# An FFT convolution with a gated expert: spectrum stored as row-pair tiles with real and imaginary parts on the free axis, corner turns scattered on the write, and the first spectrum started beside kernel generation

## Chip, cores, metric

The kernel runs on 1 core of one Trainium2 chip. The metric is device microseconds of one execution. A number called "span" is the length of the profiled execution inside the trace; the device time of the same execution is about 2 us more. Engines: PE is the matrix engine, PEld its weight loads, DVE VectorE, ACT ScalarE, POOL GpSimdE, SP SyncE (here it only issues transfers).

## The reference

```python
def reference(u, A, B, C, log_dt, Dskip, w_r, w_gate, w_up, w_down):   # u: 1 x 2048 x 512, names shortened
    xn = layernorm(u)
    # S4 convolution: K[d, l] = Re sum_n C dt B exp(dt A l), then y = irfft(rfft(xn) * rfft(K)) + xn * Dskip
    s = s4_by_fft(xn, ...)
    # the token with the largest xn @ w_r goes through one SwiGLU expert, its row is updated
    upd = scatter(silu(x_sel @ w_gate) * (x_sel @ w_up) @ w_down * sigmoid(r))
    return u + s * silu(xn + upd)
```

The work has these parts, whose names return below. **Generation** makes K on DVE (chains GG, TT; products QQ) and PE, and copies it to tile KT. The **K turn** writes KT to DRAM and reads it back as KT2. The **forward FFT** takes XN0 to AT, through DRAM to BT, and to U2. A **spectrum** (one for each half of the 512 columns, 8 groups each) multiplies KT2 by the table W into PSUM (a K product), copies that to K2T, multiplies by U2 on DVE into PAB, applies the inverse table FA (an inverse product), copies to ZT and writes that to DRAM; DD reads it back, turned. The **expert** gives UPD (its output row) and OTM (where it goes). A **gate** is silu(XN0 + UPD at its row); a **tail** finishes the inverse FFT, adds the skip term XN0 x Dskip, multiplies by the gate and adds the residual XR. There are 8 gates and a first and a last tail.

## The kernel before

Every operation is entered in a graph, and a list scheduler written in the kernel gives each engine a fixed order. A bias raises an operation's priority. The order is static: an engine whose next instruction waits does nothing else. Memory and PSUM banks are also dependences: an operation that overwrites something waits for its last reader. PSUM is the memory that PE writes its products to; the kernel uses eight banks of it, in four pairs.

```python
            cand = [n for n in avail[e] if ready[n.i] <= t]
            n = max(cand, key=lambda n: n.bl + n.bias)       # bl: longest path to the end
```

```python
        AT = place("AT", [128, 2, 8, 512], BF16)
        o_b = cur[0]
        BT = place("BT", [128, 2, 33, 256], BF16)
        F2T = place("F2T", [128, 32, 128], BF16)
        end_u = cur[0]
        W = place("W", [128, 32, 5, 128], BF16, o_u)            # over AT and BT
        FA = place("FA", [128, 32, 2, 128], BF16, o_u + 40960)
        ...
        U2S = [place(f"U2S{h}", [128, 32, 256], BF16) for h in range(2)]
```

```python
        # forward FFT, after kernel generation
            g.dma(SP, [(dap(SA, 8 * pc * 512, [[32 * 512, 128], [1, 4096]]), sap(AT, ...))])       # contiguous write
        ...
                    pr.append((sap(BT, 64 * ri + 32 * bp, 32, ...),                                # 512-byte gather
                               dap(SA, ..., [[512, 32], [32 * 512, nm], [1, 256]])))
        ...
        g.dma(AC, [(FA[:], t_fa.ap()...)])
        for h in range(2):                                       # halves (Re, Im) swapped across partitions
            g.dma(SP, [(U2S[h][0:64, :, :], U2[64:128, h, :, :]), (U2S[h][64:128, :, :], U2[0:64, h, :, :])])

        def spec(h, tg):
            pp = tg % 2
            ...   # 20 K products into PSUM pair pp, copied to K2T
            us = (U2[:, h, 4 * tg:4 * tg + 4, :], U2S[h][:, 4 * tg:4 * tg + 4, :])
            for x in range(2):
                po = PAB[:, pp, x]
                g.V(lambda e, x=x, po=po: e.tensor_tensor(out=po, in0=us[x], in1=ko, op=ALU.mult), ...)
            for t4 in range(4):
                for x in range(2):
                    mms.append((o, FA[:, t, x, :], PAB[:, pp, x, t4, :], x == 0, x == 1))   # 128 rows
            ...   # copied to ZT; one write of ZT for two groups

        def zturn(h):
            pr = []
            for bp in range(2):
                for ri in range(2):
                    pr.append((sap(DD[h], 64 * bp + 32 * ri, 32, 0, [[256, 32], [1, 256]]),
                               dap(SZ[h], (64 * ri + 32 * bp) * 32 * 256, [[256, 32], [32 * 256, 32], [1, 256]])))
            g.dma(SP, pr)
```

Of the kernel before, what the change touches and what calls it, by code (L numbers as in the profile page):

```python
# [49 lines left out]
class _Graph:  # L50
# [3 lines left out]
    def __init__(self, nc):  # L54
        self.nc = nc
        self.ctx = ExitStack()
        self.nodes = []
        self.active = []
        self.dram_bits = {}
        self.ndram = 0  # L60
        self.cache = {}
        self.sbuf = {}

# [64 lines left out]
    def add(self, eng, fns, outs, ins, ns, lat=0.0, dma=False, nbytes=0, bias=0.0, after=(), name=""):  # L128
# [45 lines left out]
    def V(self, fn, outs, ins, n, mode=1, **kw):  # L174
        return self.add(DV, [fn], outs, ins, (60 + n / mode) / 0.96, **kw)

    def A(self, fn, outs, ins, n, **kw):
        return self.add(AC, [fn], outs, ins, 230 + 0.833 * n, **kw)

    def M(self, mms, **kw):  # L180
        fns, outs, ins, ns = [], [], [], 0.0
        for o, l, r, st, sp in mms:
            tp = (_pstart(l), _pstart(o))
            fns.append(lambda e, o=o, l=l, r=r, st=st, sp=sp, tp=tp: e.matmul(o, lhsT=l, rhs=r, start=st, stop=sp, tile_position=tp, skip_group_check=True))  # L184
# [5 lines left out]
            ns += max(58.0, nn / 2.0)  # L190
        return self.add(PE, fns, outs, ins, ns, lat=60.0, **kw)

    def dma(self, eng, pairs, **kw):
        fns, outs, ins = [], [], []
        nd = 0
        nb = 0
        for dst, src in pairs:
# [6 lines left out]
            run = list(dst.ap)[-1][1] if list(dst.ap)[-1][0] == 1 else 1  # L204
            run2 = list(src.ap)[-1][1] if list(src.ap)[-1][0] == 1 else 1
            nd += cnt // max(1, min(run, run2))
            nb += cnt * mybir.dt.size(dst.dtype)
        return self.add(eng, fns, outs, ins, 60.0 * len(pairs) + 1.3 * nd, dma=True, nbytes=nb, **kw)

    def schedule(self):  # L210
# [5 lines left out]
        for n in reversed(nodes):  # L216
            t = n.ns + n.lat + (2000.0 + n.nbytes / 250.0 if n.dma else 60.0)
            n.bl = t + max([s.bl for s in succ[n.i]], default=0.0)
# [10 lines left out]
        while done < len(nodes):  # L229
# [14 lines left out]
            if n.dma:  # L244
                dma_free = max(dma_free, n.end) + n.nbytes / 250.0
# [102 lines left out]

def _pstart(ap):
# [3 lines left out]
def _tables():  # L353
# [30 lines left out]
    ONES = np.zeros((128, 128))  # L384
    ONES[0] = 1.0
    T["cf"] = [("IDENTF", IDENT), ("ONESF", ONES), ("LIDXB", LIDXB), ("CF", CF)]
# [4 lines left out]
    F2T = np.zeros((128, 32, 128))  # L391
    FA = np.zeros((128, 32, 2, 128))
    for t in range(32):
        if t == 0:
            ka, kb = 64 * k1, 32 + 64 * k1
        else:
            ka, kb = t + 64 * k1, (64 - t) + 64 * k1
        for half, kk in ((0, ka), (1, kb)):
            a = tp * np.outer(l1r, kk) / P
            c, s = np.cos(a), np.sin(a)  # L400
            sg = -1.0 if (half == 1 and t > 0) else 1.0
            isr = (ri == 0)[:, None]
            F2T[:, t, 32 * half:32 * half + 32] = np.where(isr, c, sg * s)
            F2T[:, t, 64 + 32 * half:96 + 32 * half] = np.where(isr, -s, sg * c)
        if t == 0:
            F2T[:64, 0, 64] = (-1.0) ** l1r[:64]
            F2T[64:, 0, :] = 0.0
        kin = np.concatenate([ka, kb])
        ang = tp * np.outer(kin, l1r[:64]) / P
        c, s = np.cos(ang), np.sin(ang)  # L410
        if t > 0:
            cj = np.concatenate([np.ones(32), -np.ones(32)])[:, None]
            FA[:64, t, 0, :64] = c
            FA[64:, t, 0, :64] = -c
            FA[:64, t, 1, :64] = -s
            FA[64:, t, 1, :64] = -s
            FA[:64, t, 0, 64:] = cj * s
            FA[64:, t, 0, 64:] = -cj * s
            FA[:64, t, 1, 64:] = cj * c
            FA[64:, t, 1, 64:] = cj * c  # L420
        else:
            for half in range(2):
                rr = slice(32 * half, 32 * half + 32)
                ri_ = slice(64 + 32 * half, 96 + 32 * half)
                co = slice(64 * half, 64 * half + 64)
                FA[rr, 0, 0, co] = c[rr]
                FA[ri_, 0, 0, co] = -c[rr]
                FA[rr, 0, 1, co] = -s[rr]
                FA[ri_, 0, 1, co] = -s[rr]
            FA[0, 0, 0, :64] *= 0.5  # L430
            FA[0, 0, 1, :] = 0.0
            FA[64, 0, 0, :] = 0.0
            FA[64, 0, 1, :] = 0.0
            FA[64, 0, 0, :64] = 0.5 * (-1.0) ** l1r[:64]
# [9 lines left out]
    W = np.zeros((128, 32, 5, 128))  # L444
    for t in range(32):
        if t == 0:
            ka, kb = 64 * k1, 32 + 64 * k1
        else:
            ka, kb = t + 64 * k1, (64 - t) + 64 * k1
        kin = np.concatenate([ka, kb])  # L450
        ang = tp * ((ls[:, None] * kin[None, :]) % P) / P
        full = np.concatenate([np.cos(ang), -np.sin(ang)], axis=1)
        if t == 0:
            full[:, 64] = (-1.0) ** ls
        for l in range(L):
# [3 lines left out]
            W[rr, t, tt] += full[l]  # L459
# [4 lines left out]
def build(nc, A_u, A_A_re, A_A_im, A_B_re, A_B_im, A_C_re, A_C_im, A_log_dt, A_Dskip,  # L464
# [21 lines left out]
    SA = g.dram("scr_a", 128 * 32 * 512)  # L486
    SK = [g.dram(f"scr_k{h}", 128 * 32 * 64) for h in range(2)]
    SKE = [g.dram(f"scr_e{h}", 256) for h in range(2)]
    SZ = [g.dram(f"scr_z{h}", 128 * 32 * 256) for h in range(2)]

    with g.ctx:
        cur = [0]

        def place(name, shape, dt, off=None):
# [3 lines left out]
            nb = (nb + 63) // 64 * 64  # L498
# [5 lines left out]

        XN0 = place("XN0", [128, 16, 512], BF16)
        o_u2 = cur[0]
        U2 = place("U2", [128, 2, 32, 256], BF16)
        KT2 = place("KT2", [128, 2, 5, 256], BF16)
        KT = place("KT", [128, 2, 33, 64], BF16)
# [664 lines left out]
```

## Time and profile before

| | before |
|---|---|
| device time, median of 3 | 304.55 us (303.21 to 305.95) |
| span of the profiled execution | 301.4 us |
| busy PE / DVE / ACT | 159.4 / 171.7 / 141.5 us |

No engine is busy for more than 57% of the span, so the share of busy time decides nothing; the stages do. The first fence is the page of the kernel before: the busy line, and the span cut into 40 slices of 7.5 us (a digit is the busy share in tenths; PEclk is the clock granted to PE in tenths of full speed; DMA is the mean share of the 16 DMA engines).

```profile
PE 159.4 (53%) x2067; PEld 98.3 (33%) x2067; DVE 171.7 (57%) x437; ACT 141.5 (47%) x158; POOL 0.2 (0%) x4
...
DVE  1699599999999992479650000030144446356073
...
PEclk9999999999995555855875799659789999975555
DMA  8999700000000002086899959999856649837925
```

DVE is nearly full in slices 3 to 15, while DMA does nothing from slice 6 to 15; in slices 22 to 28 DMA is full and DVE nearly idle. The next fence is the table by stage of the kernel before (start:end in us, length, busy us of each engine with its number of instructions, granted clock, DMA share, GB/s).

```profile
8.00:110.00 102.00, 32.30 (x566) 20.09 (x566) 95.49 (x282) 44.51 (x51) 0.00 (x0) 0.91 0.31 79
...
162.00:215.00 53.00, 33.02 (x323) 22.51 (x322) 3.57 (x6) 23.80 (x24) 0.00 (x0) 0.79 0.97 232
215.00:254.00 39.00, 38.94 (x309) 30.62 (x310) 16.82 (x27) 25.15 (x25) 0.00 (x0) 0.92 0.65 156
```

The chain of waits of the kernel before (start, length, what; each step was released by the one before it) names the long waits:

```profile
148.15 13.55 DMA BT<-scr_a
...
187.04 27.97 DMA FA<-c_fa
...
276.74 10.04 DMA DD_117<-scr_z
```

Three waits for transfers are on the chain: 13.6 us for BT (512-byte reads), 28.0 us for FA (W and FA can load only after BT is dead, and the swap goes along with them), and 10.0 us for DD. Between them the spectra are limited by PE. The PE timeline (start, length, shape, count) gives one group:

```profile
228.24 2.35 PE L184 MATMUL PB<-KT_51,W 128*128 128x256 bf16 x20
230.43 1.04 PE L184 MATMUL PB<-PAB,FA 128*128 128x256 bf16 x8
231.30 2.35 PE L184 MATMUL PB<-KT_51,W 128*128 128x256 bf16 x20
```

A group takes 231.30 - 228.24 = 3.06 us, of which the eight inverse products take 1.04 us.

### The profile page before, as it was taken

The numbers are of one execution on the slowest core, as the hardware profiler recorded it, in microseconds if no ns is written. First come the engines' busy times: TensorE is split into PE (matmuls) and PEld (weight loads), VectorE is DVE, ScalarE is ACT, GpSimd is POOL, SyncE is SP. The second block draws the span as 40 slices with busy tenths as digits, with TensorE's granted clock in tenths as the row PEclk, the third lists the DMA queues.
The fourth block names the chain that finished last, engine by engine and source line by source line (L and its number), as shares of the span: only waits on it lengthen the run. The fifth ranks groups of instructions, "written<-read, shape, count | busy, mean of one in ns | idle before, by whom it ended". The sixth has DMA issues, their size and how long they took to land.

```text
span 301.4 us, 4934 instructions
## 1 busy us (share of the span) xinstructions
PE 159.4 (53%) x2067; PEld 98.3 (33%) x2067; DVE 171.7 (57%) x437; ACT 141.5 (47%) x158; POOL 0.2 (0%) x4
## 2 busy tenths in 40 slices
PE   0017434100150657773734675567499999774092
PEld 0013321000140435321533453345168886321020
DVE  1699599999999992479650000030144446356073
ACT  1009973000096465988782476324176667630000
POOL 0000000000000000000000000000000000000000
PEclk9999999999995555855875799659789999975555
DMA  8999700000000002086899959999856649837925
GB/s 171 203 210 395 266 0 0 2 1 0 0 5 0 0 2 108 37 348 191 244 190 189 251 115 257 221 386 204 146 107 193 129 155 239 179 138 165 210 61 125
DMA packets 43751, 44.05 MB, mean 146 GB/s; under 512 B 13168, under 2 KB 39760, under 8 KB 42192
## 3 DMA queue, kind: packets, MB, share of 16 engines
q1 hardware_dynamic: 41712, 34.92, 49.6%
q10 hardware_dynamic: 2016, 8.81, 10.4%
q8 instruction: 16, 0.26, 0.4%
q14 instruction: 7, 0.06, 0.1%
HBM read 27.99 MB, written 11.54 MB: 131 GB/s over the span
## 4 chain that ended last, share of the span: by engine, by line
DVE 30%; PE 29%; DMA 21%; ACT 12%; SPq 4%; issue 2%; ACTq 0%
PE PB L184 29%; DMA FA<-c_fa 9%; DVE TT L760 5%; DMA BT<-scr_a 4%; SPq L198 4%; DMA DD_117<-scr_z 3%; DVE JNK L874 3%; DMA LD_66<-in_A_log_dt_dram 3%; ACT EE L697 2%; ACT U_50 L997 2%; DVE QQ L719 2%; DVE QQ L718 2%; DVE GG L762 2%; ACT AT L971 1%; DVE GG L764 1%
## 5 line engine op out<-in xcount | busy, mean ns | idle before, releaser
L184 PE MATMUL PB<-XN_49,CB 32*64 32x512 bf16 (+1 forms) x97 | 29.2, 549 | 39.1 <-ACT AT L971 22.0
L184 PE MATMUL PB<-KT_51,W 128*128 128x256 bf16 x320 | 42.3, 294 | 7.9 <-ACT K2T L1033 5.7
L1037 DVE TENSOR_TENSOR PAB<-U_50,K2T 128x1024 bf16<-128x1024 bf16 x16 | 11.1, 692 | 57.2 <-PE PB L184 37.0
L184 PE MATMUL PB<-CB,AD 128*128 128x256 bf16 (+1 forms) x96 | 19.3, 362 | 38.6 <-DVE AD L650 21.7
L184 PEld LDWEIGHTS PB<-KT_51,W 128*128 128x128 bf16 x320 | 33.2, 105 | 15.3 <-ACT K2T L1033 6.6
L971 ACT ACTIVATE AT<-PB 128x512 bf16<-128x512 f32 x32 | 18.1, 632 | 28.4 <-DVE XN_49 L867 17.5
L184 PE MATMUL PB<-QQ,GG 128*20 128x33 bf16 x1024 | 20.5, 249 | 17.0 <-DVE GG L764 9.3
L805 ACT ACTIVATE KT<-PB 128x264 bf16<-128x264 f32 x16 | 21.7, 1355 | 14.9 <-PE PB L184 14.4
L1033 ACT ACTIVATE K2T<-PB 128x1024 bf16<-128x1024 f32 x16 | 16.2, 1022 | 20.2 <-PE PB L184 11.2
L1047 ACT ACTIVATE ZT<-PB 128x1024 bf16<-128x1024 f32 x16 | 16.4, 1024 | 18.0 <-PE PB L184 16.5
L184 PEld LDWEIGHTS PB<-CB,AD 128*128 128x128 bf16 x96 | 9.6, 130 | 46.3 <-DVE AD L650 21.9
L184 PEld LDWEIGHTS PB<-QQ,GG 128*20 128x20 bf16 x1024 | 17.7, 125 | 20.6 <-DVE GG L764 10.1
L184 PEld LDWEIGHTS PB<-XN_49,CB 32*64 32x64 bf16 (+1 forms) x97 | 6.3, 114 | 55.1 <-ACT AT L971 28.4
L184 PE MATMUL PB<-PAB,FA 128*128 128x256 bf16 x128 | 19.2, 300 | 6.2 <-DMA FA<-c_fa 5.7
L760 DVE TENSOR_TENSOR TT<-GG,ZB 128x512 bf16<-128x512 bf16 (+2 forms) x48 | 21.6, 485 | 0.3
L997 ACT ACTIVATE U_50<-PB 128x1024 bf16<-128x1024 f32 x16 | 15.6, 1052 | 10.4 <-PE PB L184 8.6
L1088 DVE TENSOR_TENSOR TF<-PB,G_112 128x512 bf16<-128x512 f32 x16 | 11.0, 688 | 14.0 <-PE PB L184 14.0
L697 ACT ACTIVATE EE<-PB 128x1024 bf16<-128x1024 f32 x16 | 15.4, 1051 | 4.9 <-PE PB L184 4.8
L1037 DVE TENSOR_TENSOR PAB<-U2S_107,K2T 128x1024 bf16<-128x1024 bf16 x8 | 5.5, 684 | 20.7 <-DMA U2S_107<-U_50 20.7
L184 PEld LDWEIGHTS PB<-PAB,FA 128*128 128x128 bf16 x128 | 13.0, 106 | 10.4 <-DMA FA<-c_fa 6.0
L184 PE MATMUL PB<-BT,F2T 128*128 128x256 bf16 (+1 forms) x70 | 10.7, 306 | 10.1 <-DMA BT<-scr_a 6.5
L859 DVE BATCH_NORM_STATS2 ST<-X_78 128x6 f32<-128x512 bf16 x16 | 10.7, 686 | 5.6 <-DMA X_78<-in_A_u_dram 5.5
(130 smaller groups left out, 229.0 us busy)
## 6 DMA issues: line engine op xcount, KB each, us to landing
W<-c_w ACTq DMA_DIRECT2D x4, 1280.0 KB, 11.3
scr_a<-AT SPq DMA_DIRECT2D x4, 1024.0 KB, 3.9
scr_z<-ZT SPq DMA_DIRECT2D x8, 512.0 KB, 3.0
BT<-scr_a SPq DMA_DIRECT2D x4, 528.0 KB, 11.9
U2S_107<-U_50 SPq DMA_DIRECT2D x2, 1024.0 KB, 14.3
FA<-c_fa ACTq DMA_DIRECT2D x1, 2048.0 KB, 28.0
U2S_108<-U_50 SPq DMA_DIRECT2D x2, 1024.0 KB, 25.3
XR<-in_A_u_dram SPq DMA_DIRECT2D x8, 256.0 KB, 4.5
```

The lines of the kernel that those rows point to most:

```text
L184: fns.append(lambda e, o=o, l=l, r=r, st=st, sp=sp, tp=tp: e.matmul(o, lhsT=l, rhs=r, start=st, stop=sp, tile_position=tp, skip_group_chec ...
L198: fns.append(lambda e, dst=dst, src=src: e.dma_start(dst, src))
L697: r.append(g.A(lambda e, o=o, s=s, src=src: e.activation(out=o, in_=src, func=ACT.Exp, scale=(-8.0 if s == 0 else 8.0)), [o], [src], 1024, ...
L760: g.V(lambda e, zb=zb, o=o: e.tensor_tensor(out=o, in0=src, in1=zb, op=ALU.mult), [o], [src, zs], 256 * m, 2)
L805: g.A(lambda e, src=src, dst=dst: e.activation(out=dst, in_=src, func=ACT.Copy), [dst], [src], 264)
L859: g.V(lambda e, b=b: e.bn_stats(ST[:, b, :], X0[:, b, :]), [ST[:, b, :]], [X0[:, b, :]], 512)
L971: g.A(lambda e, o=o, bk=bk: e.activation(out=o, in_=PB[:, bk, :], func=ACT.Copy), [o], [PB[:, bk, :]], 512)
L997: g.A(lambda e, o=o, sv=sv: e.activation(out=o, in_=sv, func=ACT.Copy), [o], [sv], 1024)
L1033: g.A(lambda e: e.activation(out=ko, in_=sv, func=ACT.Copy), [ko], [sv], 1024)
L1037: g.V(lambda e, x=x, po=po: e.tensor_tensor(out=po, in0=us[x], in1=ko, op=ALU.mult), [po], [us[x], ko], 1024, 2)
L1047: g.A(lambda e: e.activation(out=zs, in_=sv2, func=ACT.Copy), [zs], [sv2], 1024)
L1088: g.V(lambda e, sv=sv, gv=gv, tv=tv: e.tensor_tensor(out=tv, in0=sv, in1=gv, op=ALU.mult), [tv], [sv, gv], 512)
```

## The change

Its intent is to use the idle DMA of 40 to 110 us for the forward FFT's turn, to remove the swap, and to let spectrum, gates and tails overlap with each other. A corner turn goes through DRAM: before, it was written in long runs and gathered in 512-byte runs when read; now it is scattered in short runs when written, so that the read has long ones.

```diff
-        o_b = cur[0]
-        BT = place("BT", [128, 2, 33, 256], BF16)
+        K2T = place("K2T", [128, 2, 2, 2, 256], BF16)
+        PAB = place("PAB", [128, 2, 2, 2, 2, 256], BF16)
+        NRING = (cur[0] - o_s) // 3072
+        WRING = [place(f"WRING{i}", [128, 1536], BF16, o_s + 3072 * i) for i in range(NRING)]   # expert weights, same memory
@@ forward FFT: entered before the expert, with a high bias
+        g.bias = 3e5
         for pair in range(8):
...
-            g.dma(SP, [(dap(SA, 8 * pc * 512, [[32 * 512, 128], [1, 4096]]), sap(AT, 0, 128, 4096 * (pc % 2), [[1, 4096]]))])
+                    pr.append((dap(SA, (64 * ri + 32 * bp + 4 * pair) * 32 * 512, [[512, 32], [32 * 512, 4], [1, 512]]),
+                               sap(AT, 64 * bp + 32 * ri, 32, 2048 * (pair % 2), [[512, 4], [1, 512]])))
+        for mg in range(4):
+            g.dma(SP, [(BT[:, 8 * mg:8 * mg + 8, :], dap(SA, 8 * mg * 512, [[32 * 512, 128], [512, 8], [1, 512]]))])
@@ spectrum
-            g.dma(SP, [(U2S[h][0:64, :, :], U2[64:128, h, :, :]), (U2S[h][64:128, :, :], U2[0:64, h, :, :])])
+                kp = 1 if h == 0 else tg % 2                    # PSUM pair of the K products
+                ip = 3 if h == 0 else 2                         # PSUM pair of the inverse products
...
+                tt(po[:, 0], us, ko, MUL, 1024, 2)
+                for ro in range(2):
+                    tt(po[:, 1, :, ro], us[:, :, ro], ko[:, :, 1 - ro], MUL, 512, 2)
+                        for par in range(2):
+                            rs = slice(64 * par, 64 * par + 64)
+                            mms.append((PB[:, 2 * ip + par, 256 * u2:256 * u2 + 256], FA[rs, 2 * tg + u2, min(x, 2), :], po[rs, ty, u2, ro, :],
+                                        x == 0, x == 3))        # 64 rows, twice as many
...
+                        pr.append((dap(SZ[h], ((2 * bp + ri) * 32 + 4 * tg) * 8192, [[256, 32], [8192, 4], [1, 256]]),
+                                   sap(ZT, 64 * ri + 32 * bp, 32, 1024 * zs, [[256, 4], [1, 256]])))    # four issues a group
+            for ig in range(4):
+                g.dma(SP, [(DD[h][:, 8 * ig:8 * ig + 8, :], dap(SZ[h], 8 * ig * 256, [[8192, 128], [1, 2048]]))])
@@ the order in which the graph is built at the end
+        g.bias = 0.0
+        spec(0)
+        g.bias = 1e5
+        nextphase()
+        kpair(2)
+        g.bias = 0.0
+        expert_tail()                                           # down weights (ring), down product in PSUM bank 7, UPD, OT
+        g.bias = 1e5
+        kpair(3)
+        g.bias = 0.0
+        extra(0)
+        g.bias = 2e5
+        kturn(1)
+        spec(1)
+        g.bias = 0.0
+        extra(1)
+        gates()                                                 # all in PSUM pair 3
...
         skipmul(0)                                              # XN0 *= Dskip, in place
+        tail(0)
         skipmul(1)
-        tail(0)
         tail(1)
```

Cut here: new tables F2T, FA and W in the pair layout, a square root on DVE in place of ACT, KT with the fastest axis contiguous, explicit loads of the ACT tables, and other duration estimates in the scheduler.

## The prediction

> **What bounds the kernel now.** No engine is busy over 57% (busy table: DVE 171.7, PE 159.4, ACT 141.5 us of 301.4). The table by stage shows that stages follow one another:
> - 8-110 us: DVE 95.5 of 102 us (layer norm, powers, G chains, Q products); DMA idle from 40.
> - 110-162: forward FFT copies, second half of kernel generation; write and 512-byte reads of BT 139.6-161.7 (chain of waits: 13.6 us for BT).
> - 162-215: W and FA share memory with BT and load only after U2; the chain waits 28.0 us for FA, the U2S swap (4 MB) beside it.
> - 215-254: both spectra, 3.06 us per group of 20+8 matmuls at clock 1.0 (PE timeline).
> - 265-287: last ZT, write, 10.0 us for DD; the second tail takes until 301.4.
>
> **What changes.**
> 1. Forward FFT, U2, W and FA move under the DVE-bound generation, where DMA is idle: the waits at 139-162 and 187-215 go (about 50 us of the chain).
> 2. Re/Im on the free axis removes the U2S swap and 0.5 MB of FA. DVE pays 0.69+2x0.42 instead of 2x0.69 us per group, +2.5 us in all. Half-height matmuls double in number; I expect pairs to overlap (the Trainium skill, "TensorE: Matmul & The Clock Gate", Part 3: disjoint tiles run concurrently; here eight 64x32 matmuls over DD took 0.40 us together).
> 3. Scatter on write: reads get 8 and 4 KB runs. DD comes in four pieces and the tail starts on the first: gap 22 -> about 9 us.
> 4. Square root on DVE: about 38 small operations of 0.18-0.2 us, +7 us on the DVE chain. KT copies (1.36 us x16, strided writes) should shorten to about 0.5 us, off the path.
> 5. The first spectrum runs beside generation of the second half; gates, residual load and first tail beside the second spectrum.
>
> **New chain.** DVE work before the end of generation: 128 us before, less 2, plus 7, plus about 8 of the first spectrum's 12: 141/0.94 = 150, from 7.5 us on: 157. KT copies and turn (130.9 to about 142 before): 13, to 170. The second spectrum also waits for the first to free K2T/PAB, and for the down weights, which load into the same ring only after the first: estimated start 176. Eight groups at 3.06 plus disturbance: 27, to 203. DD: 9. Last tail: 14, as before. Sum 226 us.
>
> **Clock.** The skill (same page, Part 1) says that a little-used PE falls to half clock. The slices agree: 0.5 at 97-112 us and after 270. At half clock a group takes about 6 us, so the overlapped first spectrum could take 49 us and end at 183: the main upward risk.
>
> **Prediction: 226 us, 80% range 209 to 247.** Faster by over 2%: 0.97; within 2%: 0.02; slower: 0.01.
>
> **Right if:** no wait for FA or BT over 5 us on the chain; no U2S issues; DMA busy at 60-120 us; DVE 180 us in total, dense to about 155; first-half K2T copies before the last KT copy; PE over 85% busy in the second spectrum; DD wait under 10 us.
> **Wrong if:** the second spectrum's first K2T copy waits long for the down weights; PABxFA matmuls take over 1.3 us a group at clock 1.0 (no pairing); DVE idle over 15 us before 150; ZT waits for scr_z writes (512-byte scatter limiting).
>
> **What would make it wrong.** Half clock throughout; SyncE's queue blocking on a write while a needed read stands behind it; the ring serialising the two spectra; or, downward, an order that ends generation by 145.

## The result

| | before | after |
|---|---|---|
| device time, median | 304.64 us (303.21 to 305.95, 4 runs) | 266.94 us (264.59 to 267.03, 4 runs) |
| ratio of the fast runs | | 0.8745 (95%: 0.8683 to 0.8807) |
| span, profiled execution | 301.4 us | 262.5 us |
| busy PE / DVE / ACT | 159.4 / 171.7 / 141.5 | 162.4 / 175.7 / 123.5 us |

A ratio is the mean time of one kernel's fast runs over that of the other's in the same rounds, so it is not quite the ratio of the medians that are quoted. The changed kernel was run again later on another chip: 266.84 us (265.55 to 267.85), ratio 0.868. The kernel before had medians of 304.6 to 306.9 us in all sets.

The change is clearly faster, and clearly slower than the forecast: 226 us was expected, 247 was the upper end. The page of the changed kernel (slices of 6.6 us):

```profile
PE 162.4 (62%) x2254; PEld 95.1 (36%) x2254; DVE 175.7 (67%) x499; ACT 123.5 (47%) x154; POOL 0.2 (0%) x4
...
DVE  1599999999999999985999124222135471115993
...
PEclk9999755555555595775698899999799998555555
DMA  4999400624679200093555599952965343800354
```

DVE is full or nearly so from slice 3 to 22 (but for slice 19), and DMA now works in slices 8 to 14. At the right end PE is granted half clock (5 in PEclk) in the last six slices, in the first two of them next to a nearly idle DVE. The table by stage:

```profile
110.00:133.00 23.00, 16.43 (x437) 12.43 (x428) 18.64 (x52) 18.36 (x24) 0.00 (x0) 0.70 0.59 170
133.00:154.00 21.00, 15.00 (x354) 11.76 (x350) 12.11 (x31) 11.24 (x15) 0.00 (x0) 0.92 0.61 230
...
218.00:239.00 21.00, 13.19 (x28) 2.59 (x27) 4.97 (x8) 7.46 (x8) 0.00 (x0) 0.57 0.34 112
239.00:262.50 23.50, 17.86 (x146) 3.87 (x146) 17.10 (x33) 0.00 (x0) 0.00 (x0) 0.50 0.38 90
```

The chain of waits of the changed kernel:

```profile
146.45 7.99 DMA FA<-c_fa
...
161.47 7.74 DMA scr_z<-ZT
...
182.39 4.18 DMA WRING_86<-in_B_w_down_dram
...
225.65 2.23 PE PB L186 x4
227.90 1.03 ACT G_115 L643
...
238.98 16.92 PE PB L186 x127
```

BT and DD have left the chain, and the wait for FA went from 28.0 to 8.0 us. New are a wait for a write of ZT (7.7 us), a wait for the expert's down weights (4.2 us), and from 215 us on an alternation of gate products (1.36 us, from 222 us on 2.23 us) and the gates' ACT (1.03 us), and then 16.9 us of tail products without a break. One group of the second spectrum in the PE timeline:

```profile
199.45 2.36 PE L186 MATMUL PB<-KT_51,W 128*128 128x256 bf16 x20
201.74 1.05 PE L186 MATMUL PB<-PAB,FA 64*128 64x256 bf16 x16
202.72 2.36 PE L186 MATMUL PB<-KT_51,W 128*128 128x256 bf16 x20
...
222.86 0.60 PE L186 MATMUL PB<-UPD,OTM 16*128 16x512 bf16 x1
...
248.43 0.61 PE L186 MATMUL PB<-DD_114,CB 64*32 64x256 bf16 x8
```

The sixteen half-height inverse products take 1.05 us, as long as the eight full ones before (1.04), so the pairs do overlap, and a group takes 202.72 - 199.45 = 3.27 us. The line at 222.86 is a gate product of the stretch after the second spectrum, at half clock: 0.60 us, where the same shape took 0.39 us at 217 us. The last line is where the last tail begins to use DD.

The forecast's sum can be laid beside the trace, step by step (the trace's column gives the place from which a step is read; both columns in us from the start):

| step of the forecast | forecast | trace of after | error of the step |
|---|---|---|---|
| DVE's work for generation ends | 157 | 143.8 | -13.2, not in the sum below |
| KT copied and turned, 13 us allowed | 170 | last read of KT2 issued at 169.7, landed by 174.7 | about 0 to +5, not in the sum below |
| second spectrum starts (its first K2T copy) | 176 | 186.4 | +10.4 |
| its end (last ZT copy), 27 us allowed | 203 | 218.3 | +4.9 (31.9 for 27) |
| last tail starts, 9 us allowed for DD | 212 | 248.4 | +21.1 (30.1 for 9) |
| end, 14 us allowed | 226 | 262.5 | +0.1 |

The first two rows cancel: DVE was 13 us early, and the copies and the turn took some 26 to 31 us instead of 13 (the last KT copy is at 149.1, but the reads of KT2 were issued only from 164.3 on). The errors of the other rows add up to 36.5 us (10.4 + 4.9 + 21.1 + 0.1); 4.4 us more are the device time over the span and the scatter of the runs. The last DD read was issued at 222.7 us and no read of it took over 7.0 us, so DD was there by 230: it is not DD that held the last tail from 230 to 248, but the gates (to 239.0) and the first tail (9.5 us) before it.

The DVE timeline of the changed kernel shows what made the second spectrum longer than its eight groups:

```profile
187.87 0.69 DVE L615 TENSOR_TENSOR PAB<-U_50,K2T 128x1024 bf16<-128x1024 bf16 x1 [2.67 <-PE PB L186]
194.30 2.04 DVE L615 TENSOR_TENSOR PAB<-U_50,K2T 128x512 bf16<-128x512 bf16 x5 [5.74 <-PE PB L186]
```

After the first PAB piece of the second spectrum DVE is idle for 5.7 us, released by PE: the next piece overwrites memory of the ring in which the last down weights lie, and PE multiplies those only at 193.5 us, after 40 K products that its order puts first.

### The profile page after: what moved, and what is told of

The parts are those of the page before. It is cut to its first block, busy times and chain, and to the rows that moved or that the text cites. A ratio compares the mean times of both kernels' runs of the same rounds, so it can differ in the third digit from the quotient of the medians.

```text
span 262.5 us, 5486 instructions
## 1 busy us (share of the span) xinstructions
PE 162.4 (62%) x2254; PEld 95.1 (36%) x2254; DVE 175.7 (67%) x499; ACT 123.5 (47%) x154; POOL 0.2 (0%) x4
## 4 chain that ended last, share of the span: by engine, by line
DVE 46%; PE 30%; DMA 10%; ACT 8%; SPq 2%; issue 2%; DVEq 0%
PE PB L186 30%; DVE TT L615 8%; DVE QQ L615 7%; DVE GG L615 4%; DVE JNK L808 4%; DVE ST L763 4%; ACT G_115 L643 3%; DVE XN_49 L620 3%; DMA FA<-c_fa 3%; DMA scr_z<-ZT 3%; DMA LD_67<-in_A_log_dt_dram 2%; ACT EE L643 2%; SPq L205 2%; DVE ZB L615 2%; DVE AD L626 2%
## 5 line engine op out<-in xcount | busy, mean ns | idle before, releaser
L615 DVE TENSOR_TENSOR PAB<-U_50,K2T 128x512 bf16<-128x512 bf16 (+1 forms) x48 | 21.9, 508 | 42.3 <-PE PB L186 36.1
L186 PE MATMUL PB<-XN_49,CB 32*64 32x512 bf16 (+2 forms) x98 | 33.1, 603 | 26.5 <-ACT G_115 L643 7.8
L615 DVE TENSOR_TENSOR TT<-GG,ZB 128x512 bf16<-128x512 bf16 (+2 forms) x64 | 27.4, 470 | 0.5
L643 ACT ACTIVATE U_50<-PB 128x1024 bf16<-128x1024 f32 x16 | 16.5, 1029 | 18.0 <-PE PB L186 18.0
L186 PE MATMUL PB<-PAB,FA 64*128 64x256 bf16 x256 | 16.8, 270 | 9.8 <-ACT ZT L643 6.2
L615 DVE TENSOR_TENSOR XN_49<-XN_49,DSKB 128x1024 bf16<-128x1024 bf16 x8 | 5.2, 688 | 19.2 <-PE PB L186 19.2
L615 DVE TENSOR_TENSOR GG<-TT 128x256 bf16<-128x256 bf16 (+2 forms) x56 | 16.4, 334 | 0.4
L186 PEld LDWEIGHTS PB<-PAB,FA 64*128 64x128 bf16 x256 | 11.2, 94 | 14.7 <-ACT ZT L643 7.6
L615 DVE TENSOR_TENSOR QQ<-QQ,EE 128x1024 bf16<-128x1024 bf16 x24 | 16.2, 681 | 0.4 <-ACT QQ L643 0.4
L643 ACT ACTIVATE G_115<-PB 128x1024 bf16<-128x1024 f32 x8 | 8.2, 1024 | 15.0 <-PE PB L186 15.0
L186 PE MATMUL PB<-BT,F2T 128*64 128x256 bf16 x128 | 13.2, 343 | 1.3 <-ACT U_50 L643 1.3
## 6 DMA issues: line engine op xcount, KB each, us to landing
XR<-in_A_u_dram SPq DMA_DIRECT2D x8, 256.0 KB, 11.5
```

Source lines behind the costliest of these rows:

```text
L186: fns.append(lambda e, o=o, l=l, r=r, st=st, sp=sp, tp=tp: e.matmul(o, lhsT=l, rhs=r, start=st, stop=sp, tile_position=tp, skip_group_chec ...
L615: g.V(lambda e: e.tensor_tensor(out=o, in0=a, in1=b, op=op), [o], [a, b], n, mode)
L643: nd = g.A(lambda e: e.activation(out=o, in_=i, func=func, **kw), [o], ins, n + (110 if "bias" in kw else 0), after=[ph["pre"]] if tab els ...
```

## The experiments

Theory A: the gates and the first tail stand behind the second spectrum instead of beside it, because the operations they depend on come late in the static order and in the order of memory, and this is most of the error. Rival B: the first spectrum comes too late, since its inputs are late, and the rest only follows. Rival C: the memory that the expert's weights and K2T/PAB share (the ring) makes the two spectra serial. The experiments are all edits of the changed kernel except one. They ran on four chips; as the kernel before agrees within 1% between them and the changed kernel within 0.1%, medians from different chips are compared below, but nothing under 1% is read from them. A run over 1.5% above the fastest of its own kernel counts as slow; where that leaves out runs, the table names the fast ones.

| run | edit | median us (range) |
|---|---|---|
| changed kernel, twice | | 266.9 and 266.8 (264.6 to 267.9) |
| e1_expert_first | router, gate, up early | 263.0 (262.7 to 263.4) |
| e7_expert_whole | and the down product before the first spectrum | 260.6 (259.4 to 261.4) |
| e5_gates_first | gates above the second spectrum | 249.8 (248.4 to 251.2; three fast runs, one slow of 416) |
| e8_expert_gates | e7 and e5 | 255.3 (254.7 to 256.1) |
| e9_gates_two_pairs | gates alternate between two PSUM pairs | 259.3 (254.8 to 260.5); fast: 254.8 |
| e2_down_own | down weights in memory of their own | 258.0 (254.1 to 261.4); fast: 254.1, 256.3 |
| f1_ring_gates | e2 and e5 | 251.4 (250.2 to 251.8) |
| e10_no_overlap | K products only after generation | 285.7 (284.6 to 286.4) |
| e4_fft_late | forward FFT at the lowest bias (its turn stayed early all the same, see below) | 280.5 (279.7 to 282.9) |
| h1_gates_in_first | gates beside the first spectrum, first tail beside the second | 248.0 (246.7 to 249.2) |
| h2, h4, h5 | h1 with transfers issued elsewhere | 249.4, 248.0, 250.0 (h5: one slow; fast: 247.6 to 250.0) |
| h3, f2 | corner turn of Z by reads, on h1 and on f1 | 258.3, 254.1 (f2: two slow; fast: 250.2, 253.7) |
| b1_no_swap | kernel before without the swap | 295.1 (290.7 to 296.4); fast: 290.7, 294.8; before in that set 305.2, but its only fast run 295.2 |

### e5: the gates first

```diff
+            g.bias = 3e5                      # expert: UPD, OT
             cp(UPD[:], PB[0:16, 7, :], 512)
...
+        g.bias = 3e5
+        gates()
         g.bias = 2e5
         kturn(1)
         spec(1)
         g.bias = 0.0
         extra(1)
-        gates()
```

> After the change, with only the gates (and the last steps of the expert) ahead of the second spectrum in priority; the down weights still load into the ring after the first spectrum. In after the eight gate steps take 24 us (215-239) behind the second spectrum, 3.34 us each: 2.2 us of PE at half clock plus 1.0 of ACT in one PSUM pair, one after the other. Theory A (order): they fit between the second spectrum's groups at about 1.4 us of PE each; that spectrum ends about 7 us later (217 -> 224), the first tail waits for the end of DD or nothing, 24 us go: net -15 to -18 us, 267 -> about 250. Rival B (gates are PE work that has to be paid wherever it stands): the second spectrum gets longer by nearly 20 us, time within 2%.

Measured: 249.8 us, the median of three fast runs, 17.1 less than the changed kernel. The profiled execution was not usable: it took 416 us, with a granted clock of 1.0 in the records but K products of 682 ns where 273 ns are usual; it is left out. So the kernel was run again for one look.

> The same kernel as e5_gates_first, once more for a profile, because the profile of that run fell in a slow state (414 us, matmuls of 0.68 instead of 0.28 us); its timed runs were 248 to 251. The theory that the gates were exposed behind the second spectrum expects here: gate copies on ACT between the K2T copies of the second spectrum, that spectrum's last ZT by about 225 instead of 218, no stretch of gate steps alone, end of the trace at about 246.

Measured: 253.4 us in its one run, so of unknown state, span 250.9. The PE timeline of e5b shows the gates inside the second spectrum, at full clock, and the chain of waits what comes after the last of them:

```profile
203.94 2.36 PE L186 MATMUL PB<-KT,W 128*128 128x256 bf16 x20
206.13 0.38 PE L186 MATMUL PB<-XN,CB 128*128 128x512 bf16 x1
...
207.40 1.05 PE L186 MATMUL PB<-PAB,FA 64*128 64x256 bf16 x16
```

```profile
227.32 18.04 PE PB L186 x138
```

The last gate ends at 227.3 us, where it was 239.0, and then both tails run as one block of 18.0 us. Theory A is right about the gates. The first tail has not moved beside anything.

### e9: two PSUM pairs for the gates

```diff
-                    mms.append((PB[:, 6 + b2, :], IDENT, XN0[:, 2 * k + b2, :], True, False))
+                    mms.append((PB[:, 2 * gp_ + b2, :], IDENT, XN0[:, 2 * k + b2, :], True, False))   # gp_ = 3 - k % 2
```

> After the change, gates left behind the second spectrum, but alternating between two pairs of PSUM banks, so that PE works on one step while ACT copies the other. In after a step takes 3.34 us (2.23 PE at half clock, then 1.02 ACT plus 0.1). If the stretch is long because PE and ACT take turns in one pair: 8 steps of 2.2 us at half clock, or 1.4 at full clock if PE then counts as busy: 24 us become 11 to 18, time 267 -> 253 to 260. If the stretch is PE work that costs the same anyway: no change over 3 us.

Measured: 259.3 us over four runs, 8 less than the changed kernel; only one of them is fast by the rule, at 254.8, 12 less. So some 8 to 12 of e5's 17 us come with the gates still behind the second spectrum, if ACT and PE need not take turns on one pair. The profiled run counts as slow.

### e2 and f1: the ring

```diff
+        WDB = [place(f"WDB{i}", [128, 1536], BF16, o_k + 3072 * i) for i in range(4)]   # where DD1 will be
...
-                    sl = ring(...)            # down weights
+                    sl = WDB[k]
+                    g.dma(SP, ...)
...
         kpair(2)
-        expert_tail()
         kpair(3)
+        g.bias = 2e5
+        expert_tail()
```

> After the change, with the down weights in memory of their own (the place of DD of the second half, free until then) and the expert's last part moved behind the generation; gates still behind the second spectrum. If the ring holds the second spectrum up: its first inverse matmul comes at about 186 instead of 195 (the first spectrum's last PAB read is at 183 and its K is ready by 174), the rest follows 9 us earlier: 267 -> about 258. If another wait takes its place (KT2 of the second half behind ZT's writes on SyncE's queue, or the clock): within 2% of 267.

Measured: 258.0 us over four runs, 9 less, as expected; the two fast runs are at 254.1 and 256.3, 12 less (ratio to before 0.833). So Rival C has a part. The edit also moves the expert's last part behind the second half of generation; the two were not run apart.

f1 is e2 and e5 together.

> Gates moved into the second spectrum (worth 17 us alone) and the down weights in a buffer of their own (worth 9 us alone), together. If the two waits stand one behind the other on the chain (ring, then gates): about 242 us, 236 to 247. If the gains hide one another, as the expert and gates gains did: 249 to 254, no better than the gates alone. The profile should show no stretch of gate matmuls alone, and the second spectrum's first inverse product at about 187 (195 in the changed kernel).

Measured: 251.4 us. The gains of 17 and 9 to 12 us do not add at all. The chain of f1 tells why:

```profile
199.47 2.20 DVE OTM L616
...
226.22 18.22 PE PB L186 x131
```

The second spectrum's first inverse product starts at 191.2 us (198.1 in e5b), but OTM, which the gates need, is made at 199.5 us and the last gate ends at 226.2: the same places as in e5b (200.4 and 227.3). The down product, whose weights were long there, runs at 194.7 us. It writes PSUM bank 7, which the first spectrum's last ZT copy reads until 190.1 us, and its place in PE's order is after the second spectrum's first group. So the ring was one of several holds on the same chain, and freeing it moved the second spectrum but not the gates.

### e1, e7, e8: the expert earlier

e1 raises the bias of router, gate and up; e7 also enters `expert_tail()` before the first spectrum; e8 adds the order of e5.

> After the change, with the priority of the expert's router, gate and up steps raised and nothing else. Theory A (order): in the trace of after, PSUM bank 7 is used by the expert from 77 to about 121 us, so eight of the sixteen U2 copies (those in banks 6 and 7) come only at 126-147, and W and FA, whose memory BT and F2T hold, land only at 152-154. Raised, the expert should leave bank 7 by about 100; the last U2 copy comes at about 120 instead of 147, FA lands before 140 instead of 154.4. The instruction order still puts seven of the first spectrum's eight groups behind the generation (149), so it should end at about 174 instead of 184: about 10 us, 267 -> 257. Rival B (clock and contention: PE at half clock and shared with generation sets the pace): FA lands earlier, but the first spectrum still ends past 182 and the time stays within 2% of 267.

Measured: 263.0 us. PSUM bank 7 is the expert's until 121 us, and U2's last eight copies, which use banks 6 and 7, run from 126 to 148 us in the changed kernel; W and FA overwrite BT and so wait for them. In e1 the last of these copies ends at 122. But the last KT copy moves from 149.1 to 157.1 us: ACT and PE do the expert and U2 where they did generation before. The first spectrum's last ZT copy ends at 182.9 instead of 184.4 us. This is what became of Rival B's gain.

> As e1_expert_first, and the down projection too comes before the first spectrum, so the ring is empty when K2T and PAB take its place. Theory A: the gap from the last PAB read of the first spectrum to the first inverse matmul of the second (183 to 195 us in after, 12 us) shrinks to what the turn of the second half needs: second spectrum's first inverse matmul at about 176 instead of 195, end at about 200, gates still behind it (24 us); time 267 -> about 248. Rival C (the ring is not what the second spectrum waits for; KT2 of the second half, issued behind the writes of ZT on SyncE's queue, is): start past 185 and no more than e1 gained.

Measured: 260.6 us, 12 above what was expected. Here the last KT copy moves to 165.9 us.

> e7_expert_whole and e5_gates_first together. If both are right and add up: second spectrum from about 176, slowed by the gates to about 4.6 us a group, end at about 208, first tail beside its end, last tail and DD behind it: 267 -> about 230, near the prediction of 226. If the losses hide one another, it is no better than the better of the two.

Measured: 255.3 us, some 25 above what was expected and 5 slower than e5 alone. In e8 PE's order puts products of the first spectrum ahead of generation's last products and waits there 4.7 us for KT2 and 4.5 us for PAB, so generation ends at 171 us. A priority that is too high does the same harm in a static order as one too low.

### e10 and e4: what the overlap is worth

e10 lets the K products of the first spectrum depend on the last KT copy.

```diff
-                g.M(mms)
+                g.M(mms, after=ktn)          # ktn: the last KT copy; second half of generation entered before spec(0)
```

> After the change, with the first spectrum forbidden to start before the last KT copy of the generation (it waits for it), the forward FFT still early. The change's third part says that the first spectrum runs beside the generation. In after only three K products and no inverse matmul of it come before the last KT copy (149.1), since FA lands at 154.4. If the overlap is thus worth nothing yet: within 1.5% of 267 (the three K products, 7 us of PE, come while it would wait for FA anyway, or move behind it). If it is worth what the prediction gave it: 15 us or more slower.

Measured: 285.7 us, 18.8 slower. This cannot be booked as the worth of the overlap. In the changed kernel the K products of only three of eight groups, and no inverse product, ran before the last KT copy or beside it, and that copy is at 147.8 us in e10, hardly earlier. What moved is the order around it: FA was issued at 161.8 instead of 146.4 us, and the chain of e10 has 8.6 us for scr_e and the reads of KT2 behind it, up to 176.6. The two causes were not taken apart.

e4 gives the forward FFT the lowest bias.

> The changed kernel with the forward transform at the lowest bias, so that it starts where the scheduler has nothing better, as in the kernel before. If the early start (filling the idle DMA at 40 to 110 us) is what took the FA and BT waits off the chain: back to 285 to 300 us, with BT and FA waits on the chain. If those waits went because of the smaller traffic (no swap) alone: within 2% of 267.

Measured: 280.5 us, 13.6 slower, below the range expected. But the edit did not make the forward FFT's turn late: the scheduler gives a free engine whatever is ready, and the reads of BT were issued at 75.9 us, as in the changed kernel (75.7). What came later is the end of the forward FFT: the last U2 copy ends at 156.6 instead of 147.8 us and FA was issued at 155.2 instead of 146.4. In front of the first inverse product PE's order then has a K product that waits 8.3 us for KT2, a read whose issuing took 11.5 us, so that the first inverse product starts at 176.0 us (154.5 in the changed kernel). So the 13.6 us are the price of a late end of the forward FFT and of what it met. That no wait for BT or FA above 3 us is on e4's chain says nothing about the early start, which e4 did not take away; what the early start is worth was not measured.

### b1: the swap, in the kernel before

```diff
-            g.dma(SP, [(U2S[h][0:64, :, :], U2[64:128, h, :, :]), (U2S[h][64:128, :, :], U2[0:64, h, :, :])])
...
-            us = (U2[:, h, 4 * tg:4 * tg + 4, :], U2S[h][:, 4 * tg:4 * tg + 4, :])
+            us = (U2[:, h, 4 * tg:4 * tg + 4, :], U2[:, h, 4 * tg:4 * tg + 4, :])
```

> The kernel before without the U2 swap, U2 used in its place (wrong result on purpose). The 4 MB of the swap share the queues with W and FA, whose wait is 28 us on the chain. If the swap is what makes that wait long: 12 to 16 us faster (about 290). If W and FA alone fill the wait: within 1% of 304.

Measured: 295.1 against 305.2 us (result wrong, relative error 0.03). By the rule for slow runs only one of the seven runs of the kernel before in this set is fast, at 295.2 us, the lowest of that kernel in any set, against 290.7 and 294.8 us of b1's fast runs. How large the gain in time is, 10 us or 2, is therefore not settled; what follows is read from the traces. FA landed in 9.5 us where it took 28.0 beside the swap, and the first inverse product moved from 215.1 to 198.4 us. The two fences are from the view of tile FA, first of the kernel before, then of b1:

```profile
DMA to landing us min/median/max: 28.0/28.0/28.0
```

```profile
DMA to landing us min/median/max: 9.5/9.5/9.5
```

Of 16.7 us gained there, 8.4 are left at the end of the profiled executions (span 293.0 for 301.4). The rest is given back after the spectra: both tails run one after the other at the end of b1, while before the first one ran in front of the wait for DD. The swap's traffic is the reason for the long FA wait.

### h1: all holds at once

The reading after f1 was this. Four things held the gates and the first tail: the ring; PSUM bank 7, in which the down product is made; PSUM pair 3, in which the gates are made, both held by the first spectrum to its end; and XN0, which `skipmul` overwrites and every gate reads, so that no tail can start before the last gate. h1 takes the first three away. Pairs 0 and 2 are free once generation has ended.

```diff
+        WDB = ...                                      # as e2
-                    mms.append((PB[0:16, 7, :], FT[...], sl[...], fc == 0, fc == 10))
+                    mms.append((PB[0:16, 4, :], FT[...], sl[...], fc == 0, fc == 10))     # and OT in bank 4
-                    mms.append((PB[:, 6 + b2, :], IDENT, XN0[:, 2 * k + b2, :], True, False))
+                    mms.append((PB[:, 2 * gp_ + b2, :], IDENT, XN0[:, 2 * k + b2, :], True, False))   # gp_ = 2 * (k % 2)
...
         kpair(3)
+        g.bias = 2e5
+        extra(0)                                       # in bank 5
+        expert_tail()
+        gates()
         kturn(1)
         spec(1)
```

> The changed kernel as it is, beside the next three on one chip: 264 to 268.

> Theory: three things hold the gates and with them the first tail (it overwrites XN0, which every gate reads) behind the spectra: the ring, the PSUM bank of the down product (7, which the first spectrum uses to its end), and the gates' PSUM pair (3, the same). Here the down weights have memory of their own, and the down product, the outer products and the gates use PSUM pairs 0 and 2, free once generation has ended; the gates may run beside the first spectrum and the first tail beside the second. If this is where the 41 us between forecast and result went: 236 to 245, no stretch of gate matmuls alone, DD matmuls of the first half before the second spectrum's last ZT. If the gains again only move into another wait, as with the ring freed and the gates first: 248 to 254.

Measured: the control 266.8, h1 248.0 us (ratio to before 0.807, control 0.868). This is outside the 236 to 245 of the theory, at the edge of the rival's range. The trace shows both at work. The PE timeline of h1:

```profile
159.82 0.38 PE L186 MATMUL PB<-XN,CB 128*128 128x512 bf16 x1
...
210.38 0.40 PE L186 MATMUL PB<-DD,CB 64*32 64x256 bf16 x8
...
219.32 1.05 PE L186 MATMUL PB<-PAB,FA 64*128 64x256 bf16 x16
232.54 0.61 PE L186 MATMUL PB<-XN,CB 128*128 128x512 bf16 x1 [12.17 <-DMA DD<-scr_z]
```

The gates now run from 159.8 us between the groups of the first spectrum; the first tail's products (DD) run from 210 us between those of the second, at full clock, 0.40 us instead of 0.61. The second spectrum's last product is at 219.3 us. Then PE is idle for 12.2 us until DD of the second half is there. Table by stage of h1:

```profile
154.00:187.00 33.00, 32.86 (x277) 21.05 (x277) 15.30 (x28) 20.75 (x21) 0.00 (x0) 1.00 0.65 146
187.00:218.00 31.00, 28.74 (x337) 20.41 (x334) 17.30 (x39) 15.82 (x17) 0.00 (x0) 1.00 0.49 139
```

From 154 to 218 us PE is busy 61.6 of 64 us at full clock. This gives the reason why the forecast's end of the second spectrum, 203 us, was not reached even with gates and first tail beside the spectra. After the last KT copy PE must still do the spectra (16 groups of 3.27 us less 2.36 us for each of two groups' K products done early, 47.6 us), the gates (8 x 4 products at 0.32 us from start to start, 10.2 us) and the first tail (8 x 0.65 = 5.2 us). An estimate from these durations is 63 us, so from 154 on: 217. Measured: the last inverse product starts at 219.3 and ends at 220.4 us. For 203 us some 14 us more of the spectra would have had to run before 154. In the changed kernel PE was busy for 31.4 of the 44 us from 110 to 154; 7.1 of these (3 x 2.36) were K products of the first spectrum already, so about 20 us were free for it, and FA, without which no inverse product can run, landed only at 154.4. The forecast put a whole spectrum there, some 26 us.

### h2, h4, h5: who issues the transfers; h3, f2: the corner turn by reads

In h1 the chain between 202 and 232 us consists for the most part of issues on SyncE and of transfers. The timeline of SyncE in h1:

```profile
219.28 1.98 SPq L205 DMA_DIRECT2D out_dram<-XR  x4
221.31 2.05 SPq L205 DMA_DIRECT2D scr_z<-ZT  x4
223.40 1.98 SPq L205 DMA_DIRECT2D out_dram<-XR  x4
225.42 2.06 SPq L205 DMA_DIRECT2D scr_z<-ZT  x4
228.81 1.76 SPq L205 DMA_DIRECT2D DD<-scr_z  x4
```

An issue takes about 0.45 us and four are needed for a group. From 219 us on the queue is full: the output writes of the first tail stand between the last writes of ZT, and the reads of DD come after all of them. The last ZT copy was done at 221.4, its write was issued at 225.4. h4 gives the residual loads and output writes to GpSimdE, h5 also half of each group's ZT writes; h2 gives GpSimdE the K turn only.

```diff
-                    g.dma(SP, pr).final = True
+                    g.dma(PO, pr).final = True          # h4, h5: output writes, residual loads
-                g.dma(SP, pr)                           # ZT writes
+                    g.dma((SP, PO)[bp], pr)             # h5
-            g.dma(SP, pr)                               # K turn
+            g.dma(PO, pr)                               # h2
```

> The previous kernel with the K turn issued by GpSimdE instead of SyncE, so that the ZT writes of the first spectrum do not stand behind the turn's reads (the 8 us wait for scr_z at 161 to 169). If that wait is on the chain: 3 to 8 us faster than the previous kernel. If PE is filled by the gates there anyway: within 1%.

Measured: 249.4 us, within 1% of h1, which the rival expected.

> In the kernel with the gates in the first spectrum (248) PE stands still for 12 us between the second spectrum's last product (220.4) and the last tail (232.5), while SyncE issues: 23 ZT writes in 21.9 us from 184, the first tail's output writes between the last ones. Here the residual loads and the output writes are issued by GpSimdE. Theory, that the last ZT write and the DD reads wait for issues of other transfers on SyncE: the gap shrinks to 6 to 8 us and the time to 241 to 245. Rival, that four writes per group at 0.45 us each fill SyncE by themselves or the transfers collide in the DMA engines: within 1% of 248.

> The previous kernel with half of each group's ZT writes issued by GpSimdE, half by SyncE. If SyncE's issue rate (four writes per group of 3.3 us) is the limit: 2 to 5 us faster than the previous kernel. If the traffic itself is, or GpSimdE's slower issues (0.55 to 0.75 us each): within 1% of it.

Measured: h4 248.0 us, h5 250.0 us (one slow run of four; its fast runs 247.6 to 250.0): no gain. The chain of h4:

```profile
221.41 3.38 DMA scr_z<-ZT
224.81 3.91 DMA DD<-scr_z
```

SyncE's queue is free sooner, but the last write of ZT then takes 3.4 us (1.8 in h1's chain) and the read of DD 3.9 us, and PE still stands idle for 10.7 us before the last tail (12.2 in h1). Of the 9.7 us after the last ZT copy (219.1 us), 2.3 are issues, 3.4 the write and 3.9 the read. The DMA engines are 65% busy from 218 to 239 us. In h5 the last write of ZT stood behind four output writes on GpSimdE's queue (2.3 us), so h5 does not test the traffic alone. The Trainium skill ("DMA: Bandwidth & Descriptors", section "Issuing engines are not separate DMA queues") says that transfers issued by different engines run on the same 16 DMA engines, and that issuing from several saves only the time of issuing. h4 and h5 agree with it: the medians moved by 0.0 and +2.0 us. Why the write takes longer in h4 was not tested.

h3 (on h1) and f2 (on f1) undo the scatter of Z: ZT is written in 2 KB runs and DD gathered in 512-byte runs by 32 reads.

```diff
-  (dap(SZ[h], ((2 * bp + ri) * 32 + 4 * tg) * 8192, [[256, 32], [8192, 4], [1, 256]]), sap(ZT, 64 * ri + 32 * bp, 32, 1024 * zs, [[256, 4], [1, 256]]))
+  (dap(SZ[h], p0 * 8192 + 4 * tg * 256, [[8192, 32], [1, 1024]]), sap(ZT, p0, 32, 1024 * zs, [[1, 1024]]))      # p0 = 64 * ri + 32 * bp
-  g.dma(SP, [(DD[h][:, 8 * ig:8 * ig + 8, :], dap(SZ[h], 8 * ig * 256, [[8192, 128], [1, 2048]]))])
+  (sap(DD[h], 64 * bp + 32 * ri, 32, 8 * ig * 256, [[256, 8], [1, 256]]), dap(SZ[h], (64 * ri + 32 * bp + 8 * ig) * 8192, [[256, 32], [8192, 8], [1, 256]]))
```

> The previous kernel with the corner turn of Z undone: ZT written in 2 KB runs, DD gathered in 512-byte runs. Theory that scatter on write shortens the chain: DD's last piece takes 9 to 11 us instead of 5, and with the gates no longer standing before the tails the time rises by 3 to 6 us. Rival, that the turn costs nothing at this place: within 1%. The waits of ZT for earlier scr_z writes (5 to 8 us at 160 to 170 us) should also shrink if the 512-byte scatter causes them, which works against the rise.

> The kernel with the gates in the first spectrum, with the corner turn of Z undone: ZT written in 2 KB runs, DD gathered in 512-byte runs by 32 instead of 8 reads. Here the last DD read stands before the last tail. If scatter on write is worth what the forecast said (gap 22 to 9 us): 5 to 13 us slower than the kernel with the scatter. If it costs nothing here either: within 1%.

Measured: f2 254.1 us (250.2 to 255.1; two of the four runs are slow by the rule) against f1's 251.4 (250.2 to 251.8): not told apart. h3 258.3 us (255.1 to 258.6) against h1's 248.0: 10 us slower. So scatter on the write is worth 10 us where the last DD read stands on the chain, and next to nothing where gates and a first tail stand before the last tail, as in f1. In the changed kernel itself it was not undone. The chain of h3 ends with the issues of the reads at 0.45 us each, then 4.4 us for the last:

```profile
240.25 0.45 SPq L205
240.74 4.42 DMA DD<-scr_z
```

## Why the prediction was right and wrong

**Right.** The direction, and, as far as the traces show, its three reasons: early FFT, no swap, long reads. What each is worth was not measured in the changed kernel (b1 is an edit of the kernel before, e4 left the turn early, h3 is an edit of h1). The waits for FA and BT left the chain (28.0 to 8.0 us, which is still over the 5 us that the forecast allowed, and 13.6 us to none), no swap is issued, and DMA works from 46 us on, in the eighth slice. The pairs of half-height products overlap: 1.05 us for 16 against 1.04 us for 8; the Trainium skill ("TensorE: Matmul & The Clock Gate", Part 3) says that matmuls on disjoint tiles run concurrently, and this trace agrees. The KT copies fell from 1.36 to 0.39 us each (0.5 forecast). DVE's work was forecast well: 175.7 us against 180. One step came right by luck: DVE ended generation 13 us sooner than forecast, and KT's copies and turn took that much longer, so that KT2 was read at about the 170 us of the forecast. The last tail took 14.1 us for 14. Three of the forecast's own signs failed: the wait for FA was over 5 us, two and not eight first-half K2T copies came before the last KT copy, and DMA was idle in slices 15 to 17 (92 to 112 us).

**Wrong: item 5, "gates, residual load and first tail beside the second spectrum", and with it the sum's step from 203 to 212 us.** This is 21.1 of 36.5 us. The gates ended 21 us after the second spectrum's last ZT copy, and the first tail came after that. e5 shows that the place of the gates is worth 17 us, the better clock they have there included. The forecast never asked what the gates wait for: the down weights in the ring, the down product's PSUM bank, the gates' one PSUM pair; nor what the first tail waits for: the last reader of XN0. h1 shows it: with the down weights, the down product and the gates elsewhere, gates and first tail do run beside the spectra, at full clock.

**Wrong: "estimated start 176" of the second spectrum, and its 27 us**, 10.4 and 4.9 us. The forecast saw the ring as a risk and gave it too little: it is the 4.2 us for down weights on the chain before the start and the 5.7 us of idle DVE after it, and e2 shows 9 to 12 us for it (together with a later place for the expert's last part). The other part is item 5's first half, "the first spectrum runs beside generation": only the K products of three groups did. U2's second half waited for PSUM banks, W and FA for U2, so that the first inverse product came at 154.5 us, after generation had ended. e1 moved U2 forward and got 4 us, since generation then ended 8 us later. Beside generation there was too little room on PE for what was to be hidden there (about 20 us for 26). A third part is the 7.7 us in which the first spectrum waited for a write of ZT (161.5 to 169.2 us on the chain), one of the signs that the forecast had named for its being wrong. The residual loads, issued from 149 to 157 us, were on the way at the same time (11.5 us to landing); whether they made the write slow was not tested.

**The clock.** The forecast feared half clock in the first spectrum. It was granted 1.0 there, and 0.95 in the second. Half clock came where the forecast had not put it: in the gates and tails from 222 us on. In e5b the gates, mixed with the spectrum, have 0.39 us products; whether it is the place or the clock that gives more of e5's gain was not taken apart.

**What stays open.** What of e10's 18.8 us is overlap and what is the order of transfers; the 10.7 us between the last inverse product and the last tail in h4; what the early start of the forward FFT is worth; and why e5's first execution took 416 us. h1 and h4 are the fastest versions found (248.0 us; ratio to before 0.807 and 0.813), with e5 close to them (249.8); the forecast's 226 was not reached.

## What to carry to other kernels

Before booking work as hidden beside something, write down for each hidden operation its last input, the memory and the PSUM banks it overwrites with their last readers, and add up each engine's work in the window: here PE had about 20 us for the first spectrum where 26 were to be hidden. When a chain has several holds at the same place (ring, bank, order), taking away one moves little, and two single gains of 17 and 9 us or more can make 15 together; look for the next hold in the trace before adding gains. A priority in a static order is a trade: what is moved forward on a shared engine pushes something else back, as e1 and e8 did with generation. And look in the trace whether an edit did what it was meant to do before reading its time: e4 did not.

## What the Trainium skill lacked or had wrong

- "TensorE: Matmul & The Clock Gate", Part 1, says that some 3.4 us of sustained activity release the half clock. In the changed kernel PE ran products back to back from 239.0 to 257 us (busy 17.86 us of the stage's 23.5, with 16.9 us without a break on the chain) and was granted 0.50 throughout, 0.61 us for a 512-column product. The tail's products alternate between full tiles and eight packed 64x32 tiles; that such a mix doesn't count as activity is a guess that no run tested. It cannot be the packed tiles alone: in e9's profiled run (slow by the rule) the gates, full tiles alternating with tiles of 16 rows, ran from 217.7 to 234.0 us without a break (busy 16.30 of 16.30 us) at a granted 0.52. In h1 the same products, mixed with the spectrum's, took 0.39 to 0.40 us.
- "DMA: Bandwidth & Descriptors", section "Issuing engines are not separate DMA queues", calls the time of issuing usually small beside the transfer. Here SyncE needs 0.45 us for each issue, so 1.8 us for the four writes of a 256 KB group, which land in about 2 us each; with 16 small reads for one half (h3) the issues stand on the chain one after the other.
- "ScalarE: Activation LUTs", section "What ACT_TABLE_LOAD costs", gives 1283 ns for a load and 1380 ns of drain beside it. The load agrees (1.28 us), but no drain is to be seen in the changed kernel's chain: the load starts 0.02 us after the exponential before it ends, and the next activation 0.01 us after the load.

```profile
116.84 1.94 ACT EE L643 x2
118.80 1.28 ACT L636
120.09 1.12 ACT QQ L643
```
